# Transposing q's features by DMA instead of on TensorE for four units, and splitting the first expert's weights in two instructions instead of three

## The chip, the cores and the metric

The kernel runs on one core of one Trainium2 chip. The metric is the device time of one execution in microseconds. The kernel before takes 619.28 us (median of 3 runs, 617.71 to 622.87).

In this text PE is TensorE (PEld its weight loads), ACT is ScalarE, DVE is VectorE, POOL is GpSimd, SP is SyncE, which here only issues DMAs.

## The reference

Linear attention with random features feeds a mixture of experts in which each token goes to one expert.

```
phi(x) = exp(h - max h) / sqrt(128),  h = x @ omega.T - |x|^2 / 2    (x scaled by 64^-1/4)
q_p, k_p = phi(q), phi(k)                       # 8 x 8 heads, 576 rows, 128 features
kv  = k_p^T v;   z = sum of k_p over the rows
x   = (q_p kv) / (q_p z + 1e-6)                 # 4608 tokens of 512
e   = argmax(x @ w_gate)                        # one of 8 experts
out = gate * (1 + exp(-x @ w_output_gate[e]))^-1 * (relu(x @ w1[e]) @ w2[e])
```

## The kernel before, in words

The attention is cut into 32 *units*; unit u is one head of two batches, nine chunks of 128 rows, and has a k half and a q half. Four times eight units give the tokens of one quarter; after each quarter the tokens are routed, and *items* (one expert on up to 128 tokens, lines 1661 and 1693) run between the later units and after them.

Matmuls want their operands as pairs of 16-bit halves, a rounded one and a remainder. Units 0 to 7 are `whole`: they project q and k in 32 bits (line 629, two matmuls for each chunk and half; the squares that they need, `lo`, are made by POOL, line 601). From unit 8 on the projection uses halves of x, made by ACT (`hi`, line 544) and POOL (line 551). A projection step `pp` of three chunks fills two PSUM banks; DVE finds a minimum (line 651) and a bias (657, later 660 and 664), and ACT takes the exponentials (670), into `ef`.

The last matmul of a unit, `pn` (line 849), needs q's features transposed, as 16-bit halves, in the tile `et`. There are two ways in the code:

- Units 0 to 7: in three groups of three chunks, PE transposes in 32 bits (`tq`, line 720), ACT rounds out of PSUM (`th`, 725), DVE subtracts (`tl`, 727).
- Units 8 and up: ACT rounds the whole of q's features (`eh`, line 691), POOL subtracts (`el`, 693), into `es`, and one DMA transpose issued by SP brings both halves to `et` (`eT`, line 747).

The first expert's weights are loaded in eight quarters (line 480, 512 KB each) while the first units run. Before, each quarter is scaled in place by ACT (line 484), rounded by ACT (488), and subtracted by POOL (492). Later experts are split by `high` on ACT (line 462, scaled and rounded at once) and `low` on DVE (line 468).

All steps stand in one list written out as numbers (`ORDER`, line 131): every engine, and SP's DMA queue with it, takes its own steps in that order, and a step whose input is late holds all that stand behind it on its engine. `BANKS` lists which PSUM bank each step gets. Tiles rotate through few buffers: two of x (`xt`), v (`rawv`), `es` and `et`, so that a load waits for the last reader of the buffer. On ACT the rounding of unit 8's x (`hi`, line 544) stands ahead of unit 6's key-value halves (`kvh`, line 784), which PE's step `kt` (line 805) waits for through DVE (line 788).

Of the kernel before, what the change touches and what calls it, by code (L numbers as in the profile page):

```python
# [90 lines left out]
WHOLE = 8  # L91
ASSUMED = (4, 12, 21, 26, 31, 37)
# [235 lines left out]
def attention_moe(ctx: ExitStack, tc: tile.TileContext, kqt, kqn, v, om, wg, w1, w2, cf, cm, ci, out):  # L328
    nc = tc.nc
# [1544 lines left out]
```

## Time and profile before

| what | value |
| --- | --- |
| median of 3 runs | 619.28 us (617.71 to 622.87) |
| profiled execution, its own time | 620.54 us |
| its span, first to last instruction | 618.5 us |
| PE busy | 594.8 us (96%) |
| ACT busy | 420.6 us (68%) |
| DVE busy | 386.0 us (62%) |
| POOL busy | 376.2 us (61%) |
| mean granted clock of PE | 0.986 |

The busy times are averages over stages with different limits: the units 0 to 7 fill the first 75 us, the change to the later kind of unit and the first routing the next 45, and from 120 us on items and units share PE. Matmuls are pipelined and their ends are modelled, so a busy PE is not PE at its peak; how long a step holds PE is read from the start of the step after it.

### The profile page before, as it was taken

The page shows a single profiled execution, that of the slowest core. Times are in us where ns is not written, and L with a number is a line of the kernel's source. Part 1 is how long each engine was busy: PE and PEld are TensorE (multiplying, and loading weights), DVE is VectorE, ACT ScalarE, POOL GpSimd, SP SyncE. Part 2 cuts the span into 40 slices and gives each one's busy share as a digit, 9 for nine tenths or more (in the row PEclk, how much of TensorE's full clock was granted, in tenths as well). Part 3 has the DMA queues.
Part 4 walks back from the last instruction along what each step waited for, and adds up shares of the span by engine and source line. Part 5 has one row for each costly group of instructions (what it writes and reads, how often), then busy time and mean ns, then how long its engine had stood idle before and what let it go on. Part 6 is the DMA issues. An engine that isn't in the chain of part 4 may idle for free. (4 is left out here: it accounts for less than half of the span.)

```text
span 618.5 us, 22153 instructions
## 1 busy us (share of the span) xinstructions
PE 594.8 (96%) x8736; PEld 471.3 (76%) x8736; DVE 386.0 (62%) x1220; ACT 420.6 (68%) x978; POOL 376.2 (61%) x275
## 2 busy tenths in 40 slices
PE   8999987999999999999999999999999999999995
PEld 8999876877796777778777777778867587777775
DVE  4877699876678887657797856543693351162143
ACT  6999999779888688889958787872431341351244
POOL 2265689788977879997897889985322122121203
PEclk9999997899999999999999999999999899999999
DMA  8655688999999999989978999777586935942391
GB/s 282 196 158 159 212 274 212 233 236 257 305 251 217 254 281 242 269 188 238 304 199 251 247 192 203 171 170 222 193 176 189 245 82 109 300 117 69 104 278 50
DMA packets 146022, 128.86 MB, mean 208 GB/s; under 512 B 104286, under 2 KB 127584, under 8 KB 144608
## 3 DMA queue, kind: packets, MB, share of 16 engines
q1 hardware_dynamic: 139904, 107.45, 68.6%
q0 software_dynamic: 5984, 19.72, 10.1%
q8 instruction: 73, 1.20, 0.8%
q14 instruction: 61, 0.50, 0.3%
HBM read 83.86 MB, written 19.30 MB: 167 GB/s over the span
## 5 line engine op out<-in xcount | busy, mean ns | idle before, releaser
L1661 PE MATMUL ph<-xt,w1h 128*128 128x128 f16 (+1 forms) x2368 | 200.4, 218 | 2.2 <-ACT ef L670 0.7
L1661 PE MATMUL ph<-xt,w1l 128*128 128x128 f16 (+1 forms) x1184 | 196.6, 218 | 0.9 <-issue 0.9
L1661 PEld LDWEIGHTS <-w1h 128*128 128x128 f16 x2368 | 178.2, 98 | 9.6 <-issue 2.4
L670 ACT ACTIVATE ef<-pp,nb 128x128 f32<-128x128 f32 x576 | 163.7, 397 | 15.7 <-DVE nb L664 11.4
L651 DVE TENSOR_REDUCE pp<-pp 128x3 f32<-128x384 f32 x192 | 103.0, 557 | 35.2 <-PE pp L629 29.0
L693 POOL TENSOR_TENSOR es<-ef,es 128x1152 f16<-128x1152 f32 x44 | 104.8, 2390 | 25.8 <-ACT es L691 15.2
L1661 PEld LDWEIGHTS <-w1l 128*128 128x128 f16 x1184 | 115.2, 98 | 1.6 <-issue 1.6
L1672 DVE SCALAR_TENSOR_TENSOR hl<-ph,hh 128x512 f16<-128x512 f32 (+1 forms) x76 | 50.4, 664 | 95.2 <-ACTq L1555 53.5
L1693 PE MATMUL po<-w2h,hh 128*128 128x512 f16 x280 | 106.9, 382 | 0.4 <-ACT es L691 0.4
L1693 PE MATMUL po<-w2l,hh 128*128 128x512 f16 x280 | 106.8, 382 | 0.0
L1693 PE MATMUL po<-w2h,hl 128*128 128x512 f16 x280 | 106.7, 381 | 0.0
L1668 ACT ACTIVATE hh<-ph 128x512 f16<-128x512 f32 (+1 forms) x76 | 44.5, 591 | 85.5 <-PE ph L1661 65.7
L1693 PEld LDWEIGHTS <-hh 128*128 128x128 f16 x560 | 51.5, 98 | 53.7 <-issue 1.9
L1617 POOL DMA_INDIRECT gx<-rows,gi x38 | 39.5, 1038 | 83.3 <-ACT os L1772 34.4
L551 POOL TENSOR_TENSOR xlo<-xt,xhi 128x1152 f16<-128x1152 f32 x24 | 57.3, 2386 | 9.8 <-ACT xhi L544 8.0
L691 ACT CAST es<-ef 128x1152 f16<-128x1152 f32 x44 | 51.5, 1180 | 3.0 <-DMA et<-es 2.3
L1693 PEld LDWEIGHTS <-hl 128*128 128x128 f16 x280 | 27.5, 98 | 33.8 <-issue 0.8
L1772 ACT ACTIVATE os<-po,gx 128x512 f32<-128x512 f32 (+1 forms) x34 | 23.3, 686 | 43.5 <-PE po L1693 39.7
L849 PE MATMUL pn<-kvs,et 128*128 128x81 f16 (+1 forms) x960 | 47.9, 204 | 2.2 <-DVE nb L664 0.7
L849 PEld LDWEIGHTS <-et 128*128 128x128 f16 (+1 forms) x960 | 40.5, 101 | 9.3 <-issue 1.8
L629 PE MATMUL pp<-omh,xhi 64*128 64x128 f16 x432 | 42.9, 223 | 2.3 <-ACT ef L670 0.9
L1759 POOL DMA_INDIRECT out<-os,oi x25 | 26.6, 1065 | 27.7 <-ACT os L1772 22.9
(215 smaller groups left out, 1093.6 us busy)
## 6 DMA issues: line engine op xcount, KB each, us to landing
r<-w SPq DMA_DIRECT2D x10, 2048.0 KB
xt<-kqt SPq DMA_DIRECT2D x31, 576.0 KB
xn<-kqn SPq DMA_DIRECT2D x24, 576.0 KB
rawv<-v SPq DMA_DIRECT2D x32, 325.0 KB
rows<-xs SPq DMA_DIRECT2D x16, 576.0 KB
r<-w SPq DMA_DIRECT2D x8, 512.0 KB
ef<-w SPq DMA_DIRECT2D x2, 512.0 KB
et<-w SPq DMA_DIRECT2D x2, 512.0 KB
```

What stands on the lines that cost most here:

```text
L551: lambda t0=t0, t1=t1: nc.gpsimd.tensor_tensor(out=xl(u)[:, t0:t1], in0=xt32(u)[:, t0:t1], in1=xh(u)[:, t0:t1], op=ALU.subtract),
L629: nc.tensor.matmul(banks["pp", 2 * u + i, g][:, c, :], x[r, t], w[r, :], start=(a == 0), stop=(a == len(ops) - 1))
L651: nc.vector.tensor_reduce(out=pp[:, 3, 0:3], in_=pp[:, 0:3, :], op=ALU.min, axis=AX.X)
L670: nc.scalar.activation(ef(n)[:, c, :], banks["pp", n, g][:, c % 3, :], AF.Exp, bias=nb(n)[:, c : c + 1], scale=-SK)
L691: nc.scalar.copy(es(slot_es(n))[:, 0], ef(n))
L693: nc.gpsimd.tensor_tensor(out=es(slot_es(n))[:, 1], in0=ef(n), in1=es(slot_es(n))[:, 0], op=ALU.subtract)
L849: nc.tensor.matmul(pn[lo:hi, c - c0, :], a[:, c, lo:hi], w[:, :, b], start=(i == 0), stop=(i == len(ops) - 1))
L1617: nc.gpsimd.indirect_dma_start(out=gx(n), out_offset=None, in_=rows[0 : (j + 1) * NC * P], in_offset=bass.IndirectOffsetOnAxis(ap=tabs[gr] ...
L1661: nc.tensor.matmul(ph[:, f4, 0:w_], w[qd][:, kk, fo : fo + P], xt(n)[:, x, 0:w_], start=(a == 0), stop=(a == 3 * KC - 1))
L1668: nc.scalar.activation(hh(n)[:, sl, 0:w_], banks["ph", n, g][:, :, 0:w_], AF.Relu)
L1672: nc.vector.scalar_tensor_tensor(out=hl(n)[:, sl, 0:w_], in0=banks["ph", n, g][:, :, 0:w_], scalar=0.0, in1=hh(n)[:, sl, 0:w_], op0=ALU.ma ...
L1693: nc.tensor.matmul(po, x(n)[:, f, :], w[f // 2][:, f % 2, :], start=(f == 0 and a == 0), stop=(f == FC - 1 and a == 2))
```

## The change

- Units 2 to 5 (`TURNED`) keep the 32-bit projection, but take the other way to `et`: `tq`, `th` and `tl` go, and `eh`, `el` and `eT` come in their place.
- Each quarter of the first expert's weights is split by `high` (ACT) and `low` (DVE), as the later experts' are; the scaling in place and POOL's subtraction go.
- `ORDER` and `BANKS` are written anew. From the first routing's list of tokens on, the common steps stand in the same order; before it the weights' roundings and subtractions stand earlier, and the `pn` of units 3 and 4 later.

```diff
+TURNED = (2, 3, 4, 5)
...
-        def scale_up(which, i):
-            src, _, _, sc = quarter(which, i)
-            nc.scalar.activation(src, src, AF.Copy, scale=sc)
-
-        def rounded(which, i):
-            src, hi, _, _ = quarter(which, i)
-            nc.scalar.copy(hi, src)
-
-        def remainder(which, i):
-            src, hi, lo, _ = quarter(which, i)
-            nc.gpsimd.tensor_tensor(out=lo, in0=src, in1=hi, op=ALU.subtract)
...
-                    ("w0s", *key), ("ACT",), 0.95, lambda which=which, i=i: scale_up(which, i), after=[("w0", *key)], rank=R
-                )
-                plan.add(
-                    ("w0h", *key), ("ACT",), 0.95, lambda which=which, i=i: rounded(which, i), after=[("w0s", *key)], rank=R
+                    ("w0h", *key), ("ACT",), 0.95, lambda which=which, i=i: high(which, i), after=[("w0", *key)], rank=R
                 )
                 plan.add(
-                    ("w0l", *key), ("POOL",), 2.1, lambda which=which, i=i: remainder(which, i), after=[("w0h", *key)], rank=R
+                    ("w0l", *key), ("DVE",), 1.22, lambda which=which, i=i: low(which, i), after=[("w0h", *key)], rank=R
                 )
...
-        if whole:
+        if whole and u not in TURNED:
             def turned(g):
```

The change's lines lie 13 to 16 above those of before: its 731 is 747, its 677 is 693, its 585 is 601.

SP's queue, from behind the load of unit 5's x, before (578 loads x, 588 loads v, 480 a quarter of the weights, 923 stores rows of the result):

```order
L588 DMA rawv_988<-v 128x650
L578 DMA xt_990<-kqt 128x1152
L480 DMA r_108<-w 128x1024
L578 DMA xt_993<-kqt 128x1152
L923 DMA rows<-xs_547 128x9x128
L923 DMA rows<-xs_1040 128x9x128
L588 DMA rawv_1211<-v 128x650
L578 DMA xt_1213<-kqt 128x1152
L578 DMA xn_1215<-kqn 128x1152
```

and now:

```order
L731 DMA_TRANSPOSE et_663<-es_533 128x18x128
L731 DMA_TRANSPOSE et_910<-es_701 128x18x128
L572 DMA rawv_949<-v 128x650
L562 DMA xt_951<-kqt 128x1152
L479 DMA r_108<-w 128x1024
L562 DMA xt_954<-kqt 128x1152
L731 DMA_TRANSPOSE et_998<-es_846 128x18x128
L907 DMA rows<-xs_542 128x9x128
L907 DMA rows<-xs_992 128x9x128
L572 DMA rawv_1153<-v 128x650
L731 DMA_TRANSPOSE et_1155<-es_987 128x18x128
L562 DMA xt_1157<-kqt 128x1152
```

Unit 2's transpose stands right behind the load of unit 5's x, unit 3's behind that; unit 4's behind the load of unit 7's x, and unit 5's ahead of the load of unit 8's x (`xt_1157`, before `xt_1213`).

POOL, from the squares of unit 4 (`xn_549`) to the remainder of unit 8's x, before (880 and 884 make halves of the result, 902 sums logits):

```order
L902 TENSOR_TENSOR lga_747<-lga_747,xf_833 128x144
L880 CAST xs_1040<-xf_945 128x9x64
L902 TENSOR_TENSOR lga_747<-lga_747,xf_945 128x144
L884 TENSOR_TENSOR xs_1040<-xf_945,xs_1040 128x9x64
L601 TENSOR_TENSOR xn_1049<-xt_993 128x1152
L902 TENSOR_TENSOR lga_747<-lga_747,xf_1109 128x144
L492 TENSOR_TENSOR w2l_105<-r_108,w2h_101 128x1024
L492 TENSOR_TENSOR w1l_95<-r_107,w1h_91 128x1024
L551 TENSOR_TENSOR xlo_1309<-xt_1213,xhi_1243 128x1152
```

and now:

```order
L585 TENSOR_TENSOR xn_995<-xt_951 128x1152
L677 TENSOR_TENSOR es_846<-ef_796,es_846 128x1152
L886 TENSOR_TENSOR lga_727<-lga_727,xf_810 128x144
L864 CAST xs_992<-xf_932 128x9x64
L886 TENSOR_TENSOR lga_727<-lga_727,xf_932 128x144
L868 TENSOR_TENSOR xs_992<-xf_932,xs_992 128x9x64
L585 TENSOR_TENSOR xn_1004<-xt_954 128x1152
L677 TENSOR_TENSOR es_987<-ef_868,es_987 128x1152
L886 TENSOR_TENSOR lga_727<-lga_727,xf_1070 128x144
L535 TENSOR_TENSOR xlo_1251<-xt_1157,xhi_1187 128x1152
```

The remainders of the weights (492) are gone, and a remainder of q's features (677, before 693) follows the squares of units 6 and 7; the two of units 2 and 3 stand in the same way further up, unit 2's right behind the squares of unit 4.

PE, where unit 2's features of q were transposed, between unit 1's `pn` and unit 3's last projection, before:

```order
L849 MATMUL pn_5_565<-kvs_398,et_380 128x81
L720 MATMUL tq_1_578<-ident,ef_413 128x128 x3
L766 MATMUL kv_582<-rawv_326,ef_482 128x130 x5
L720 MATMUL tq_2_588<-ident,ef_413 128x128 x3
L766 MATMUL kv_582<-rawv_326,ef_482 128x130 x5
L629 MATMUL pp_2_625<-omf,xt_328 128x128
```

and now:

```order
L833 MATMUL pn_5_561<-kvs_397,et_380 128x81
L750 MATMUL kv_574<-rawv_326,ef_482 128x130 x10
L613 MATMUL pp_2_609<-omf,xt_328 128x128
L613 MATMUL pp_2_610<-omf,xt_328 128x128
```

The two groups of three transposes are gone and the key-value matmuls (766, now 750) follow each other.

## Rows read from the trace of the kernel before

**Rows 1.** Stretches: length, busy PE PEld DVE ACT POOL, PEclk, DMA share, GB/s.

```profile
10.00:75.00 65.00, 64.76 (x901) 60.03 (x899) 48.52 (x160) 61.70 (x183) 31.21 (x24) 1.00 0.61 190
75.00:120.00 45.00, 37.10 (x544) 32.42 (x545) 40.00 (x171) 39.48 (x118) 37.98 (x25) 0.85 0.87 234
80.00:110.00 30.00, 23.34 (x345) 20.59 (x344) 28.57 (x128) 27.85 (x79) 26.54 (x16) 0.83 0.85 229
95.00:115.00 20.00, 17.16 (x210) 15.22 (x211) 17.12 (x83) 15.83 (x47) 16.84 (x11) 0.66 0.86 220
120.00:600.00 480.00, 473.34 (x6992) 361.55 (x6990) 287.08 (x871) 307.97 (x661) 299.97 (x219) 1.00 0.84 213
```

**Rows 2.** PE in order of time: start, length, line, what, count.

```profile
31.88 0.51 PE L720 MATMUL tq<-ident,ef 128*128 128x128 f32 x3
32.23 1.28 PE L766 MATMUL kv<-rawv,ef 128*128 128x130 f32 x10
...
60.84 0.82 PE L720 MATMUL tq<-ident,ef 128*128 128x128 f32 x6
61.49 0.63 PE L849 MATMUL pn<-kvs,et 128*128 128x81 f16 x12
```

**Rows 3.** Costliest groups by form: count, busy us, mean ns of one, idle before.

```profile
L693 POOL TENSOR_TENSOR es<-ef,es 128x1152 f16<-128x1152 f32 x44 | 104.8, 2390 | 25.8 <-ACT es L691 15.2 <-issue 8.4 <-ACTq L1576 2.1
...
L691 ACT CAST es<-ef 128x1152 f16<-128x1152 f32 x44 | 51.5, 1180 | 3.0 <-DMA et<-es 2.3 <-issue 0.2
...
L468 DVE SCALAR_TENSOR_TENSOR w1l<-r,w1h 128x1024 f16<-128x1024 f32 x16 | 19.6, 1272 | 8.6 <-ACT w1h L462 8.6
...
L727 DVE TENSOR_TENSOR et<-tq,et 128x384 f16<-128x384 f32 x24 | 12.8, 549 | 2.4 <-ACT et L725 2.4
...
L725 ACT CAST et<-tq 128x384 f16<-128x384 f32 x24 | 11.4, 513 | 1.0 <-PE tq L720 1.0
...
L484 ACT ACTIVATE r<-r 128x1024 f32<-128x1024 f32 x8 | 8.8, 1102 | 0.0
L492 POOL TENSOR_TENSOR w1l<-r,w1h 128x1024 f16<-128x1024 f32 x4 | 8.5, 2132 | 0.0
```

**Rows 4.** Queue of SP in order of time: start, length of issue, line, transfer.

```profile
36.36 0.33 SPq L578 DMA_DIRECT2D xt<-kqt  x1
...
55.96 0.33 SPq L578 DMA_DIRECT2D xt<-kqt  x1
...
66.06 0.35 SPq L578 DMA_DIRECT2D xt<-kqt  x1
...
119.17 3.55 SPq L747 DMA_TRANSPOSE et<-es  x1
```

**Rows 5.** DMA engines, 119 to 125 us in 40 slices, busy tenths.

```profile
DMA  0000005999939993996999999999999922991993
```

**Rows 6.** POOL, then ACT, in order of time.

```profile
31.48 2.10 POOL L601 TENSOR_TENSOR xn<-xt 128x1152 f32<-128x1152 f32 x1 [3.65 <-PE pp L629]
...
60.41 2.11 POOL L601 TENSOR_TENSOR xn<-xt 128x1152 f32<-128x1152 f32 x1 [2.28 <-PE kv L766]
...
70.39 1.25 ACT L544 CAST xhi<-xt 128x1152 f16<-128x1152 f32 x1
```

**Rows 7.** PE, then DVE, in order of time.

```profile
43.51 1.34 PE L849 MATMUL pn<-kvs,et 128*128 128x81 f16 x30
...
73.81 0.27 PE L805 MATMUL kv<-cmt,kvs 128*128 128x128 f16 x2
...
76.88 1.03 DVE L651 TENSOR_REDUCE pp<-pp 128x3 f32<-128x384 f32 x2 [1.28 <-PE pp L629]
```

**Rows 8.** POOL at two places, then DVE beside the second.

```profile
169.72 0.48 POOL L902 TENSOR_TENSOR lga<-lga,xf 128x144 f32<-128x144 f32 x1
...
303.22 1.49 POOL L902 TENSOR_TENSOR lga<-lga,xf 128x144 f32<-128x144 f32 x1
...
302.62 5.45 DVE L468 SCALAR_TENSOR_TENSOR w1l<-r,w1h 128x1024 f16<-128x1024 f32 x4 [2.81 <-ACT w1h L462]
```

More of the change, by code (lines that the diff above doesn't have):

```diff
@@ L131 @@
 ORDER = """
[135 rows of a table removed]
[134 rows of a table added]
 """
 BANKS = """
-01234567102453165273016042306751043267430613457425134062356710264573016240615704265137531240763540613710743562347035
-16743510716346571634204765726410356741530274551472630514753026741430621506327140751620461235643154753124567346102751
-06432547130654372164507312506457236105634721406524102364736051244276503270165603257105623715027265703416720614253107
-64623154026731426753126053461752607415236407351406732510467235041672350416273504612357061423353353353353353353353353
-35335335
+01234567102453165273016042307510427430613742514037102655732460615704265137531240763540613710743562347035167435107163
+46571634204765726410356741530274551472630514753026741430621506327140751620461235643154753124567346102751064325471306
+54372164507312506457236105634721406524102364736051244276503270165603257105623715027265703416720614253107646231540267
+3142675312605346175260741523640735140673251046723504167235041627350461235706142335335335335335335335335335335335
 """
```

269 rows, old and new, of the table ORDER are left out of this document.

## The prediction

> **What bounds the kernel now.** I read the busy times by stretch first, then the waits of PE, then the order of time on each queue. From 10 to 75 us PE is busy 64.76 of 65.00 us at full clock, and steps follow each other without a gap [rows 1, 2]: here whatever PE no longer does is time. From 80 to 110 us DVE is busy 28.57 of 30.00 us, PE only 23.34 [rows 1]: the later kind of unit asks more of DVE, the first routing falls in the same place, and DVE is the bound, with ACT close behind (27.85). PE loses 45.00 - 37.10 = 7.9 us idle between 75 and 120 us, and its granted clock falls to a mean of 0.66 between 95 and 115 us, after the stretch in which it waited [rows 1]. From 120 to 600 us PE is busy 473.34 of 480.00 us [rows 1], with the same work before and after the change. So the end moves by as much as the work at 110 to 120 us moves, and the change must be costed up to there.
>
> **The change, part by part.**
>
> *PE's transposes.* Twelve groups of three go. A group holds PE from its start to the next step's: 32.23 - 31.88 = 0.35 us, and two together 61.49 - 60.84 = 0.65 us [rows 2]. Twelve by 0.34 are 4.1 us, all of it in the stretch in which PE is the bound. The 0.51 and 0.82 us that the rows give as lengths overlap the next step and aren't taken.
>
> *ACT.* Eight scalings in place (1.10 us) and twelve roundings out of PSUM (0.51) go, four roundings of 1.18 come: -8.8 - 6.2 + 4.7 = -10.3 us [rows 3]. ACT is busy 61.70 of 65 us up to 75 us, but PE doesn't wait for it there, so I cost this at nothing; the cover is PE's own work. It is slack that the new roundings use.
>
> *POOL.* Eight subtractions of 2.13 us go, four of 2.39 come: -17.0 + 9.6 = -7.5 us [rows 3]. POOL is busy 31.21 of 65 us in the first stretch; nothing for the total. But the four that come stand in a chain to `pn`, which is costed below.
>
> *DVE.* Twelve subtractions of 0.55 us go, eight of 1.27 come: -6.6 + 10.2 = +3.6 us [rows 3]. All stand before 75 us, where DVE is busy 48.52 of 65 us [rows 1]: 16.5 us of slack cover them. What isn't covered is that each, being 1.27 us long, can hold a minimum or bias behind it, and so ACT and a PSUM bank. Bounds: nothing, or 8 by 1.27. I take nothing, since PE has steps of other units to do at each place.
>
> *The new chain to `pn`.* Now q's features go ACT, POOL, SP, DMA. A transpose issued at 119.17 holds SP's queue 3.55 us [rows 4], and the DMA engines fall idle at slice 32 of 40 of a view of 6 us that begins at 119, thus at 123.8 [rows 5]: 4.6 us from issue to landing.
>
> Unit 2: POOL's subtraction stands right behind the squares of unit 4, which ran 31.48 to 33.58 [rows 6], so it ends at 36.0. The queue gets there after the load of unit 5's x, 36.36 before [rows 4], about 1 us sooner now. Issue 36.0, landing 40.6. `pn` started at 43.51 [rows 7]; five groups fewer stand ahead of it, so it is due at 41.8. That fits by a hair, with two loads ahead on the DMA engines. Bounds of the wait: 0 and 1.5 us; I take 0.5.
>
> Unit 5: its transpose stands ahead of the load of unit 8's x on SP. The load of unit 7's x was issued at 55.96 [rows 4], when PE had done unit 5's projection; the squares of unit 7 followed at 60.41 [rows 6], 4.45 us later. Now eight groups (2.7 us) and unit 3's `pn` (1.3 us by unit 2's row [rows 7]) no longer stand ahead of that point, 0.5 us of waiting does: 52.5. Squares from 56.9 to 59.0, subtraction to 61.4, transpose on the queue until 65.0. Unit 8's x was loaded at 66.06 before, and ACT began to round it at 70.39 [rows 4, 6], 4.3 us later; now 65.0 and 69.3, done at 70.5. On ACT that rounding stands ahead of unit 6's key-value halves, which PE's `kt` waits for. `kt` stood at 73.81 [rows 7]; without this it would be due at 73.81 - 4.1 + 0.5 = 70.2, with it at about 71.0 (I allow 0.5 us for the two short steps between). That is 2.8 us sooner than before. Bounds: the load can also be 1.0 us slower beside the transpose's own data, which lands at 66.0.
>
> *Units 3 and 4.* Their `pn` stand later in the new order, behind further projections, so their transposes have some 3 us to spare at the same pace; nothing.
>
> *From there on.* DVE begins its full stretch at 76.88, when the last projection of unit 7 ends [rows 7]. That moves with `kt`, 2.8 us. What DVE does from there to 110 us isn't changed, so its end moves by the same 2.8 us, and so does all that follows. That POOL loses five of its eight weight subtractions from this very stretch helps steps that wait for DVE anyway; nothing.
>
> *Sum.* The profiled execution took 620.54 us: 620.54 - 2.8 = 617.7. The median of the runs, 619.28, stands 1.26 us below that execution, which gives 616.5. Without any stall it is 619.28 - 4.1 = 615.2; with both stalls at their ends (1.0 us more at unit 2, 1.0 more at unit 8) 618.5.
>
> *A rule that speaks against it.* In the trace a logits sum of POOL takes 0.48 us alone and 1.49 us while DVE splits weights, and the four splits beside it take 5.45 us [rows 8]. The Trainium skill's page "GPSIMD Engine Reference", section "8. Key points", says that POOL shares its SBUF interfaces with VectorE and that the two contend when a DVE instruction has two SBUF inputs; such a subtraction has two, and the trace agrees, with 1.0 us more on a short step. By that rule the change puts eight such instructions among the very POOL steps that now lie in the chain; that is the second rival.
>
> **The rivals.**
>
> *The idle stretch shrinks too (faster).* If DVE isn't really the bound from 80 to 110 us, but POOL's lateness with the halves of units 9 to 11 is (POOL 26.54 of 30 [rows 1]), then five subtractions fewer, 5 by 2.13 = 10.7 us, close PE's gaps, and the clock doesn't fall. PE's 17.16 busy us between 95 and 115 us at 0.66 would be 11.3 at full clock: 5.8 us, with the 2.8 above 8.6 us, so 610.7. For it: POOL's load, and that the clock fell only after PE had waited. Against: DVE's 28.57 of 30, which the change leaves as it is.
>
> *SP's queue holds unit 8 (slower).* The price of unit 5's transpose falls on the load behind it. If its subtraction ends after 62.5 (66.06 - 3.55), that load is later than before; from 64.2 on, `kt` is later too, since it had 1.7 us to spare behind the rounding's end at 71.64. By the contention above each of four subtractions or squares in series may take 1.0 us more: 61.4 + 4 = 65.4. Then the load goes out at 69.0, the rounding ends at 74.5, and unit 8's halves are 2.9 us later than before, `kt` 1.2. I take 2.2: 621.5. For it: the chain runs in series through POOL and SP. Against: the single 1.0 us was seen for a short step, and DVE's splits are spread over 50 us.
>
> *DVE takes it all (no change).* The 3.6 us more on DVE, and the wait of minima behind 1.27 us splits, eat the 2.8 us: 619.3. Against: its 16.5 us of slack; for it: PE's banks come free only through DVE and ACT.
>
> **How the numbers follow.** The forecast has 0.54, the faster rival 0.15, the slower one 0.14, no change 0.17. The predicted time is the forecast's, 616.5; its own range is 615.2 to 618.5. The 8 in 10 run from 610.5, where half of the faster rival lies below, to 622.0, which leaves out the worse part of the slower one and a little of the rest. A measurement of this kernel can tell about 1%, 6.2 us, from no change (its three runs lie 5.2 us apart). Faster by that, below 613.1: nearly all of the faster rival and a little of the forecast, 0.16. Slower, above 625.5: only the end of the slower rival, 0.05. The same: 0.79.
>
> **What would show it.** Right: no `tq` of units 2 to 5 and PE still without gaps to 70 us; unit 2's `pn` waiting under 1.5 us for its transpose; the load of unit 8's x issued about 65.0, `kt` of unit 6 about 71.0, DVE's full stretch beginning about 74 and as long as before; the clock falling again. Wrong: a mean clock near 1.00 between 90 and 115 us and PE idle well under 7.9 us (faster rival); the load of unit 8's x after 66 us, or PE waiting for `et` for microseconds (slower rival); gaps on PE behind minima before 70 us (no change).

## The result, and the profile after

The changed kernel takes 628.43 us (median of 6 runs, 627.29 to 635.83) beside 621.74 us of the kernel before (6 runs): a ratio of 1.0143, 95% interval 1.0105 to 1.018. The forecast was 616.5 us with a range of 610.5 to 622.0, that is 0.9955 of the 619.28 us it started from. It is wrong in sign and in size. The profiled execution has a span of 625.2 us (before 618.5) and took 627.29 us.

The kernel before takes 614 us on some chips and 621 on others, so every experiment below is read as its ratio to the runs of before on its own chip, and places in the program are read as time behind one milestone, `kt` of unit 0 (the product that turns a unit's key-value state). Line numbers of other kernels differ by up to 21 from those of before. One profile, that of e7, is of a slower execution; only its part before 101 us is read.

Stretches of the changed kernel (length; busy PE, PEld, DVE, ACT, POOL; PEclk; DMA share; GB/s), which answer to [rows 1]:

```profile
10.00:75.00 65.00, 58.37 (x768) 53.65 (x770) 49.42 (x138) 48.52 (x147) 37.90 (x24) 0.95 0.75 201
75.00:120.00 45.00, 35.23 (x538) 31.09 (x535) 38.32 (x161) 40.58 (x115) 23.84 (x17) 0.92 0.90 249
80.00:110.00 30.00, 23.00 (x375) 19.65 (x374) 27.26 (x107) 27.97 (x77) 20.85 (x16) 1.00 0.90 249
...
120.00:600.00 480.00, 472.54 (x6974) 362.21 (x6973) 290.09 (x892) 309.44 (x672) 305.73 (x223) 1.00 0.85 211
...
45.00:50.00 5.00, 3.54 (x44) 3.33 (x46) 2.99 (x10) 2.88 (x9) 4.25 (x2) 0.66 0.99 190
...
60.00:65.00 5.00, 2.98 (x27) 2.59 (x28) 4.98 (x17) 3.05 (x13) 3.44 (x5) 0.87 1.03 237
65.00:70.00 5.00, 5.00 (x54) 4.76 (x53) 3.15 (x7) 4.30 (x11) 4.70 (x2) 0.79 0.98 273
```

From 10 to 75 us PE is now idle 65.00 - 58.37 = 6.6 us (before 0.24), and its granted clock, which was 1.00 in that stretch, falls to 0.66 and 0.79 in two places, that is, part of the time at 1.2 GHz and not 2.4. ACT is 13 us less busy there, in part because the window now holds less of the program; PE gains nothing by it. PE in order of time, beside [rows 7] (there `pn` of unit 2 stood at 43.51 and `kt` of unit 6 at 73.81):

```profile
41.53 2.51 PE L750 MATMUL kv<-rawv,ef 128*128 128x130 f32 x20
46.46 2.10 PE L833 MATMUL pn<-kvs,et 128*128 128x81 f16 x30 [2.42 <-DMA et<-es]
...
58.30 1.48 PE L833 MATMUL pn<-kvs,et 128*128 128x81 f16 x30
...
62.01 0.84 PE L613 MATMUL pp<-omf,xt 64*128 64x128 f32 x3 [2.16 <-issue]
64.28 3.85 PE L750 MATMUL kv<-rawv,ef 128*128 128x130 f32 x20
...
70.88 0.28 PE L789 MATMUL kv<-cmt,kvs 128*128 128x128 f16 x2
...
80.99 0.27 PE L789 MATMUL kv<-cmt,kvs 128*128 128x128 f16 x2
```

Two stops: 2.42 us at unit 2's `pn`, which waits for the DMA transpose, and 2.16 us before unit 6's projection, of which the view says only "issue". Behind each the clock is low: `pn` takes 2.10 us (1.34 before), unit 5's `kv` 3.85 (2.51 for unit 3's, at 41.53). The last row is unit 6's `kt`, 7.2 us later than before. SP's queue, beside [rows 4]:

```profile
37.05 0.33 SPq L562 DMA_DIRECT2D xt<-kqt  x1
37.49 10.30 SPq L731 DMA_TRANSPOSE et<-es  x2
...
58.23 0.33 SPq L562 DMA_DIRECT2D xt<-kqt  x1
...
69.72 2.66 SPq L731 DMA_TRANSPOSE et<-es  x1
73.22 0.34 SPq L562 DMA_DIRECT2D xt<-kqt  x1
```

Unit 2's transpose is issued at 37.49 and its data is there when `pn` starts, at 46.46: 9.0 us, not 4.6. The last row is the load of unit 8's x, 7.2 us later than before (66.06). Now the milestones, `kt` of each unit as its start behind unit 0's, in us, and unit 0's own start in the trace (worked out from the rows of that product in each trace), with the ratios:

```
        u0 at   u2     u3     u4     u5     u6     u8    ratio to before (95%)
before  21.36  15.08  24.95  32.92  43.06  52.45  72.83  1
after   22.55  14.58  28.19  33.99  48.33  58.44  78.83  1.0143 (1.0105-1.0180)
e1      20.62  14.23  26.64  32.44  46.87  56.56  76.96  1.0080 (1.0051-1.0109)
e2      21.76  15.17  28.28  36.90  47.67  57.16  77.54  1.0077 (1.0044-1.0110)
e3      22.27  14.60  26.05  31.86  48.41  58.69  79.08  1.0090 (1.0059-1.0121)
e4      21.51  14.59  23.74  33.87  48.21  58.32  78.94  1.0087 (1.0054-1.0120)
e5      21.81  14.22  22.86  32.28  45.87  55.58  75.97  1.0075 (1.0049-1.0101)
e6      22.15  14.59  23.50  32.11  45.72  56.32  76.91  1.0075 (1.0041-1.0109)
e7      22.24  15.20  25.55  37.42  48.14  57.65  78.05  1.0083 (1.0054-1.0112)
e8      22.54  14.56  26.23  32.03  49.54  61.16  82.31  1.0166 (1.0124-1.0209)
e9      21.95  14.59  23.36  30.80  42.62  54.43  75.55  1.0100 (1.0054-1.0147)
e10     21.06  14.22  22.42  29.86  41.44  53.36  74.99  1.0112 (1.0074-1.0150)
e11     23.17  15.19  25.88  35.23  50.55  61.02  81.64  1.0174 (1.0115-1.0233)
e12     22.20  14.24  22.43  30.23  41.80  55.24  78.99  1.0113 (1.0080-1.0146)
e13     21.04  14.22  22.43  29.98  41.57  51.21  78.49  1.0101 (1.0068-1.0135)
e14     20.98  14.21  22.43  29.75  41.34  53.96  79.09  1.0120 (1.0088-1.0152)
e15     22.11  14.58  23.09  30.56  42.57  58.48  82.80  1.0196 (1.0154-1.0238)
e16     21.07  14.22  22.82  29.87  41.52  51.21  72.78  1.0023 (0.9991-1.0055)
e17     21.03  14.22  22.85  30.22  42.85  52.91  74.15  1.0040 (1.0007-1.0074)
e18     22.54  14.59  23.46  32.16  43.48  54.02  78.06  1.0077 (1.0049-1.0105)
```

All that the changed kernel loses is lost before unit 6. From unit 6 to unit 8 it takes 20.39 us (before 20.38), and from unit 8 to the end 523.8 us (524.3; both are the span less the start of unit 8's `kt`).

### The profile page after: what moved, and what is told of

It reads as the page before. It is cut to its first block, busy times and chain, and to the rows that moved or that the text cites. A ratio compares the mean times of both kernels' runs of the same rounds, so it can differ in the third digit from the quotient of the medians.

```text
span 625.2 us, 22068 instructions
## 1 busy us (share of the span) xinstructions
PE 592.0 (95%) x8700; PEld 468.8 (75%) x8700; DVE 393.4 (63%) x1216; ACT 415.3 (66%) x962; POOL 374.3 (60%) x271
## 5 line engine op out<-in xcount | busy, mean ns | idle before, releaser
L677 POOL TENSOR_TENSOR es<-ef,es 128x1152 f16<-128x1152 f32 x48 | 114.3, 2391 | 29.5 <-ACT es L675 20.4
L675 ACT CAST es<-ef 128x1152 f16<-128x1152 f32 x48 | 56.2, 1180 | 1.5 <-DMA et<-es 0.7
L833 PE MATMUL pn<-kvs,et 128*128 128x81 f16 (+1 forms) x960 | 49.2, 208 | 4.6 <-DMA et<-es 2.4
L868 POOL TENSOR_TENSOR xs<-xf,xs 128x576 f16<-128x576 f32 x32 | 42.0, 1313 | 1.1
```

Source lines behind the costliest of these rows:

```text
L675: nc.scalar.copy(es(slot_es(n))[:, 0], ef(n))
L677: nc.gpsimd.tensor_tensor(out=es(slot_es(n))[:, 1], in0=ef(n), in1=es(slot_es(n))[:, 0], op=ALU.subtract)
L833: nc.tensor.matmul(pn[lo:hi, c - c0, :], a[:, c, lo:hi], w[:, :, b], start=(i == 0), stop=(i == len(ops) - 1))
L868: nc.gpsimd.tensor_tensor(out=x[:, :, P + o : P + o + D], in0=xf(u)[:, :, 0:D], in1=x[:, :, o : o + D], op=ALU.subtract)
```

## The experiments

The edits of e3 to e18 are in the order in which steps are given to an engine and in the PSUM banks that they get. Both stand in the kernel as tables of numbers, so the diffs name the steps.

**e1 and e2: each half alone.** e1 is the kernel before with the transposes moved to DMA; e2 is the changed kernel with `TURNED = ()`, so only the weights change.

```diff
 # e1, against before
+TURNED = (2, 3, 4, 5)
-        if whole:
+        if whole and u not in TURNED:
 # e2, against the changed kernel
-TURNED = (2, 3, 4, 5)
+TURNED = ()
```

> Half of the change: units 2 to 5 turn q's features by DMA as in the changed kernel, while the first expert's weights are split as before (scaled on ScalarE, rounded on ScalarE, remainder on GpSimd, each at its old place). Theory A (the loss is made where DMA transposes land late and where unit 3's products, moved behind unit 5's projections, leave VectorE's divides standing ahead of unit 5's minima): the loss stays, 625.5 to 629 us. Theory B (the loss comes from the weights' remainders, put on VectorE beside GpSimd and ahead of the minima): the loss goes, 618 to 622 us. Theory C (the transposes hold SP's queue, and the loads behind them are late): the loss stays, 626 to 629 us, and GpSimd's squares of units 6 and 7 stay as late as in the changed kernel.

> The other half: the weights in two instructions (rounding with the scale on ScalarE, remainder on VectorE) at the changed kernel's places, while units 2 to 5 turn q's features on TensorE, as before, and unit 3's products stand at their old place. Theory A: what is lost is the start alone (unit 1's turned state 1.2 us later in the changed kernel, from a remainder that stands ahead of unit 0's transposed halves), 621 to 624 us. Theory B: most of the loss, 625 to 629 us, with VectorE's remainders of 1.22 to 2.5 us ahead of minima. Theory C: no loss, 620 to 622 us.

Each half loses 0.8%, and within the intervals the two add up to the whole. That is A's and C's figure for e1 and B's for e2 (by ratio 626.7 and 626.5 us where before is 621.7); A had given e2 no more than the late start, and C nothing. C's second sign failed: in e1 POOL's squares of units 6 and 7 start at 52.14 and 60.87 us, in the changed kernel at 55.53 and 64.27. e2 shows one place where the weights cost time. DVE, POOL and ACT of e2 in order of time:

```profile
44.17 2.78 DVE L464 SCALAR_TENSOR_TENSOR w1l<-r,w1h 128x1024 f16<-128x1024 f32 x1
```

```profile
43.77 2.11 POOL L582 TENSOR_TENSOR xn<-xt 128x1152 f32<-128x1152 f32 x1 [0.23 <-DMA xt<-kqt]
```

```profile
48.19 1.66 ACT L651 ACTIVATE ef<-pp,nb 128x128 f32<-128x128 f32 x6 [1.52 <-DVE nb L638]
```

The remainder starts at 44.17 while POOL squares until 45.88, and ends at 46.95, that is 1.07 us after POOL is done; alone it takes 1.22. By these times it doesn't run slowly beside POOL, it waits for POOL's instruction to end. Behind it stand unit 4's minima, and ACT waits 1.52 us for their biases.

**e3 and e4: one stop each out of the changed kernel.**

```diff
 # e3, DVE: kvs.4, then
-xf.3 (divides of unit 3, 6 steps), mx.10.1 ... nb.11.1 (minima, biases of unit 5)
+mx.10.1, router's state, ... nb.11.1, xf.3
 # e4, PE                                   # e4, DVE
-pn.2, pp.4.2, kt.3                         -xf.2, mx.9.2 ... nb.8.2
+pp.4.2, kt.3, pn.2                         +mx.9.2 ... nb.8.2, xf.2
```

> The changed kernel with one edit: on VectorE the six steps that divide unit 3's products stand behind the minima and biases of unit 5, not ahead of them; TensorE's order, SP's and ScalarE's are untouched. Theory A: VectorE's idle 3.5 us at 55.8, ScalarE's 3.4 us at 58.1 and TensorE's 2.2 us at 62 go, and with them TensorE's lower clock at 60 to 70: 623.5 to 626.5 us. Theories B and C: 627.5 to 629 us, since the wait is only passed on.

> The changed kernel with one edit: unit 2's products stand behind unit 4's last projection and unit 3's key-value turn on TensorE, and the divides of unit 2 behind unit 4's minima on VectorE. Theory A: TensorE no longer waits 2.4 us for unit 2's transposed features, its clock stays up at 45 to 50, and unit 3's turned state comes 2.5 to 3.5 us earlier: 624 to 626.5 us if the later stop at unit 3 stays, no more than 628 if that stop grows by what was won. Theory B: 627.5 to 629. Theory C: 627.5 to 629, as the loads of units 6 to 8 are issued when they were.

e4 did at its place what theory A said, and more: unit 3 comes 4.45 us earlier (28.19 to 23.74), unit 4 only 0.1. In both, unit 5 is where it was (48.41, 48.21 against 48.33): the next stop took it. The ratios fell by 0.005, and the intervals still overlap with that of the changed kernel. For e4 that is A's second branch; e3 is a miss for A. In e3 four small copies of the router's state came up beside POOL's work. DVE of e3, then POOL:

```profile
54.70 1.57 DVE L392 TENSOR_SCALAR cnt<-cft 128x8 f32<-128x8 f32 x1
56.18 0.16 DVE L393 TENSOR_SCALAR done<-cft 128x8 f32<-128x8 f32 x1
56.26 2.34 DVE L394 COPY off<-cft 128x8 f32<-128x8 f32 x1
```

```profile
54.14 2.11 POOL L580 TENSOR_TENSOR xn<-xt 128x1152 f32<-128x1152 f32 x1 [0.97 <-DMA xt<-kqt]
56.20 2.37 POOL L672 TENSOR_TENSOR es<-ef,es 128x1152 f16<-128x1152 f32 x1
```

Copies of 8 numbers, 0.16 us each where POOL rests, take 1.57 and 2.34 us and end at 56.27 and 58.60, as POOL's instructions end (56.25 and 58.57).

**e5 to e7: all named stops out of e1, of the changed kernel, and one remainder out of e2.** e5 is e1 with both edits of e3 and e4 and the state's copies behind the minima too; e6 is the changed kernel with these and one remainder, w0l.1.2, moved; e7 is e2 with that remainder moved.

```diff
 # e6 and e7, DVE
-gl.2, w0l.1.2, kvs.3, mx.9.0 ... xf.2, w0l.1.3
+gl.2, kvs.3, mx.9.0 ... xf.2, w0l.1.2, w0l.1.3
```

> The transposes alone (weights as before, as in e1_turned_only), with both stops taken out by order alone: unit 2's products behind unit 4's last projection and unit 3's turn on TensorE, unit 2's and unit 3's divides on VectorE behind the minima of units 4 and 5, and the four small copies of the router's state behind them too. e1 lost 2.85 us at unit 2's products (waiting for the transpose) and 2.2 us before unit 6's projections, and after each TensorE ran at its lower clock (the key-value sums of unit 5 took 4.1 us). Theory A (these waits and the clock are the whole loss of this half; its saving on TensorE is real): 5 to 8 us below e1, so 611.5 to 614.5 us, level with the kernel before or up to 2 us faster. Theory C (the transposes' hold on the queue sets the pace): the later milestones stay, 618 to 620 us.

> The changed kernel with the order of e5_turned_unblocked, and the remainder of the weights' third quarter of the first matrix, which stood ahead of unit 4's minima on VectorE while GpSimd was at work, put beside the fourth quarter's, a place where GpSimd is idle. Theory A with B (each half loses by its own waits): what is left is the 1.2 us at the start and the remainders that wait for GpSimd at 63 and 69 us, 614 to 617.5 us. If the order gives nothing more than e3 and e4 gave: 618.5 to 620 us.

> The weights alone (as in e2_weights_only), with one instruction moved: the remainder of the first matrix's third quarter, which took 2.78 us in e2 and stood ahead of unit 4's first minima, goes behind unit 2's last divide, beside the fourth quarter's. In e2 the way from unit 2's turned state to unit 3's took 13.1 us, 3.2 us more than in the kernel before. Theory B (that one instruction, held while GpSimd runs, makes the loss): this way takes 10 to 11.5 us, and the time is 615.5 to 617.5 us. Against it (VectorE's sum of work is what counts, wherever it stands): 618.5 to 620 us.

None gave what A expected: by time e5 came out at C's figure, e6 and e7 at the second of their branches. The milestone of e7 did as expected (unit 2 to unit 3: 10.35 us, e2 13.11), the time didn't: the two remainders, now in a row, took 2.82 us at 49.52, and unit 3 to unit 4 went from 8.6 to 11.9 us. e5 won nothing on e1. Its PE:

```profile
48.50 0.49 PE L623 MATMUL pp<-omf,xt 64*128 64x128 f32 x4 [1.39 <-issue]
...
59.28 0.49 PE L623 MATMUL pp<-omf,xt 64*128 64x128 f32 x4 [1.91 <-issue]
61.34 3.58 PE L760 MATMUL kv<-rawv,ef 128*128 128x130 f32 x20
```

Unit 6's projection starts at 59.28; DVE's last divide of unit 3 ended at 59.18. The table of banks gives this projection the bank which that divide frees (as in the changed kernel, where the divide ran 61.42 to 61.90 and the projection began at 62.01). So the banks became theory D. The sentence on six free banks in e8's expectation counts by the order in the table; in time most of them weren't free yet, since ACT's exponentials were late too, as e8 then showed.

**e8 to e11: banks chosen anew** for the requests of units 3 to 6 (longest free first, a bank freed by a divide last), in the changed kernel, in e6, e5 and e7. A few later requests follow from these.

```diff
 # e8, bank of          (freed by)
-pp.12.0  5             (xf.3, DVE)
+pp.12.0  one that an exponential freed (ACT)
```

> The changed kernel, every engine's order as it is; only the PSUM banks that the steps of units 3 to 6 take are chosen anew: of the free banks the one that has been free longest, and one that a divide frees only if no other is free. In the changed kernel unit 6's first projections took the bank that unit 3's last divide freed (61.90 us, projections at 62.01), although six others had been free for up to 4 us, and unit 5's first ones a bank of unit 2's divide. Theory D (TensorE stops since the table of banks, made for the old order, hands it banks that late divides free): the 2.16 us before unit 6's projections go in part, unit 5's turned state 1 to 3 us earlier, 625 to 627 us where before is 621.7. Theory A (VectorE's divides ahead of the minima are what stops): no change, since the exponentials are late either way, 1.012 to 1.015 of the time before.

> e6_all_unblocked (the changed kernel with unit 2's products later, the divides of units 2 and 3 behind the minima, one remainder moved) with banks chosen as in e8_banks_only. Theory A with D (orders and banks each hid behind the other): no stop of TensorE over 1 us between 40 and 75 us but the one of unit 2, the clock stays up, and unit 8's turned state stands 72.5 to 74.5 us behind unit 0's (before 72.8, e6 76.9): 1.000 to 1.004 of the time before. If the milestone stays at 76 to 77: 1.006 to 1.009.

> e5_turned_unblocked (transposes alone, products and divides moved) with banks chosen as in e8_banks_only. e5 had 1.39 us of stop before unit 5's projections and 1.91 us before unit 6's, each ending as a divide freed a bank, and 2 to 3 us of lower clock behind them. Theory A with D: those go, unit 8's turned state 70.5 to 72.5 us behind unit 0's (before 72.8, e5 76.0): 0.994 to 1.000 of the time before. If the transposes themselves hold the pace: 1.006 to 1.009 as e5.

> e7_one_remainder_moved (weights alone, one remainder moved) with banks chosen as in e8_banks_only. In e7 unit 4's key-value sums waited 2.00 us for a bank that VectorE freed behind two remainders (49.5 to 52.3), and then ran at the lower clock (4.07 us). Theory B with D: this stop goes, unit 8's turned state 73.5 to 76 us behind unit 0's (before 72.8, e7 78.0): 1.001 to 1.005. If VectorE's added work alone sets the pace: 1.007 to 1.009 as e7.

Theory D falls: alone the new banks don't help. e11 is slower than e7, and e8, though its interval overlaps that of the changed kernel, has unit 6 2.7 us later. By ratio all four came out above both branches of what was expected. In e8 unit 6's projection stops 2.98 us, now for a bank of ACT's, as ACT's exponentials stand behind the blocked minima. With the order mended as well, unit 5 comes 41.44 us behind unit 0 in e10 and 42.62 in e9, before 43.06: up to here the transposes alone win 1.6 us, where e1 lost 3.8. The stops form a chain: minima wait behind divides on DVE, exponentials on ACT wait for the minima, banks for the exponentials, and PE for the banks. So all must go together. But unit 8 is 2.2 us late again in e10, which expected 70.5 to 72.5, and 2.7 in e9. Its SP, then its ACT:

```profile
63.04 3.94 SPq L741 DMA_TRANSPOSE et<-es  x1
67.07 0.53 SPq L572 DMA_DIRECT2D xt<-kqt  x1
```

```profile
72.64 1.15 ACT L538 CAST xhi<-xt 128x1152 f16<-128x1152 f32 x1 [3.80 <-DMA xt<-kqt]
```

**e12 to e15: the queue and the rounding of unit 8's x.**

```diff
 # e12, SP                                  # e13, ACT
-eT.5, ld.t.8, ld.n.8                       -hi.8, kvh.6, th.6.2
+ld.t.8, ld.n.8, eT.5                       +kvh.6, th.6.2, hi.8
 # e14: e10 with both.  e15: e9 with both.  All four: banks by e8's rule up to unit 8.
```

> e10_turned_unblocked_banks (transposes alone, no stops before 65 us) with one edit on SP's queue: unit 5's DMA transpose goes behind the loads of unit 8's x and its squares, not ahead of them (the banks are chosen by e10's rule up to unit 8, so that unit 7's projections no longer wait for a transposed half). In e10 the load was issued at 67.07, after 3.94 us that the transpose held the queue, though unit 6's last projection, whose buffer it takes, was done at 64.4; it landed at 72.6, and ScalarE waited 3.80 us for it with unit 6's key-value copies behind. Theory C (the queue): load issued at 64.5 to 65.5, landed near 70, unit 8's turned state 72 to 73.5 us behind unit 0's (e10 75.0, before 72.8); 2 to 3 us less than e10. If the transpose then lands too late for unit 5's products: 75 or more.

> e10_turned_unblocked_banks with one edit on ScalarE: the rounding of unit 8's x stands behind unit 6's key-value copy and second transposed third, not ahead of them (and GpSimd's remainder of it likewise; banks as in e12_queue). Theory E (what takes the gain back is ScalarE's in-order queue, held 3.80 us by a load): unit 6's turned state comes 1 to 2.5 us earlier, and unit 8's 72.5 to 74 us behind unit 0's (e10 75.0). If unit 8's projections wait for the rounded halves anyway: 74.5 to 75.5.

> The transposes alone with every stop that the traces named taken out: e12_queue's and e13_round_later's edits together. If stops by order were the whole cost of this half, its saving of 4.1 us on TensorE before 70 us must now show: unit 8's turned state 69.5 to 72 us behind unit 0's (before 72.8), the time 0.993 to 1.000 of the kernel before. If other work takes it back (the 75 to 125 us stretch, bound by VectorE): 1.002 to 1.008.

> The changed kernel with both edits of e14_turned_all on top of e9_all_unblocked_banks, so the whole change with every stop that the traces named taken out, except the remainders on VectorE that wait for GpSimd at 63 and 69 us and the one of 1.2 us at the start. Unit 8's turned state 72 to 74 us behind unit 0's, which itself is 1.0 to 1.2 us late: 0.998 to 1.005 of the kernel before. If VectorE's remainders cost by their sum: 1.007 to 1.012.

e12 came out at its second branch: behind the loads the transposed data come too late. SP, then PE of e12:

```profile
66.81 6.41 SPq L741 DMA_TRANSPOSE et<-es  x1
```

```profile
75.35 2.29 PE L843 MATMUL pn<-kvs,et 128*128 128x81 f16 x30 [3.09 <-DMA et<-es]
```

The transpose lands 8.5 us after its issue, and PE waits 3.09 us, as it does in e15 (3.10) and, by 2.57, in e14. e13 is the opposite: with the rounding behind `kvh.6`, unit 6 comes 51.21 us behind unit 0, 1.24 us ahead of the kernel before; theory E holds up to there. Then it lost 7 us, to its banks as e16 shows; the longest stop is this one on PE:

```profile
92.19 0.23 PE L623 MATMUL pp<-omh,xhi 64*128 64x128 f16 x2 [3.47 <-ACT ef L664]
```

So e14 and e15, which missed by far, are spoiled by the bank rule as well, and say nothing on the change's worth. The same may hold for e9 to e11 behind unit 6; that wasn't tested.

**e16 and e17: the banks of the changed kernel kept** wherever the same step frees them; only the first projections of the k halves of units 5 and 6 are given others, and six requests follow from that. So e16 is e5 with eight other banks and the rounding moved. e17 also leaves unit 5 on PE.

```diff
 # e16: e13 with the old table's banks, but for pp.10.0, pp.12.0 (and six that follow)
 # e17: e16 with
-TURNED = (2, 3, 4, 5)
+TURNED = (2, 3, 4)
```

> e13_round_later with the banks of the changed kernel's own table wherever a step can take the bank that the same step freed there; only the first projections of units 5 and 6 take others (those that an exponential frees, not a divide), and eight requests follow from that. Theory F (from unit 6 on e12 to e15 lost by the bank table that they were given): the stops of 0.92 and 3.47 us at 77 and 92 us go; unit 6's turned state 51 to 52 us, unit 8's 72.5 to 74.5 us behind unit 0's (e13 78.5, before 72.8), 1.000 to 1.005 of the kernel before. If unit 8's late x sets the pace whatever the banks: 75 us or more, 1.006 to 1.010.

> As e16_banks_kept, but only units 2, 3 and 4 turn q's features by DMA; unit 5 keeps TensorE, ScalarE and VectorE for it, as before, so that nothing stands on SP's queue ahead of the load of unit 8's x. Theory C (the queue and the late x8 are what is left): the load is issued within 1 us of unit 6's last projection and unit 8's turned state is 70.5 to 72.5 us behind unit 0's (before 72.8): 0.994 to 1.000 of the kernel before. If the DMA queues are busy with loads and transposes anyway: 73 to 75 us, 1.000 to 1.005.

e16 came as expected: 1.0023, not to be told from the kernel before. It isn't faster either. No run puts its order, its banks or its moved rounding into a kernel that turns on PE, so what they alone are worth isn't known. Stretches of e16:

```profile
10.00:75.00 65.00, 62.67 (x878) 57.97 (x879) 44.01 (x149) 60.60 (x173) 40.03 (x28) 1.00 0.80 228
75.00:120.00 45.00, 36.50 (x530) 31.57 (x528) 39.98 (x170) 39.40 (x117) 38.80 (x26) 0.85 0.93 241
80.00:110.00 30.00, 23.00 (x338) 20.27 (x337) 28.04 (x129) 27.45 (x77) 26.50 (x16) 0.82 0.99 238
```

It keeps PE's clock at 1.00 to 75 us; from 80 to 110 us DVE and ACT are as full as before [rows 1]. It is 1.24 us ahead of the kernel before at unit 6 and 0.05 at units 7 and 8 (the kernel before has unit 7 at 61.75, e16 at 61.70). e17 answers theory C: with no transpose ahead of it on the queue the load goes out 0.7 us sooner (66.17, e16 66.88), and from unit 5 to unit 8 it takes 31.3 us as e16 does (before 29.8): its second branch. Unit 5's transpose on the queue isn't what takes the last 1.2 us.

**e18: e16 with the weights in two instructions.**

```diff
 # e18, against e16: w0s, w0h on ACT and w0l on POOL become
+w0h (scale and round) on ACT, w0l on DVE, at e6's places
```

> The whole change (transposes, and the weights in two instructions with the remainder on VectorE) in the order and with the bank rule of e16_banks_kept; of the eight remainders one is moved to a place where GpSimd is idle, as in e6. If the weights' half lost only by the one remainder that stood ahead of unit 4's minima and by the banks: unit 8's turned state 72.5 to 73.5 us behind unit 0's, the time 1.002 to 1.005, what is left being the 1.2 us at the start. If each remainder that meets GpSimd at work, and the 1.22 us that each takes ahead of other VectorE work, is paid for: 74.5 to 76 us, 1.006 to 1.010.

1.0077 against e16's 1.0023: the weights' half keeps a price. By ratio that is the second branch, but unit 8, 78.06 us behind unit 0, is later than both branches had it. Unit 0 stands at 22.54 us, and the eleven kernels with the new weights have it at 22.25 on average, the eight with the old ones and the kernel before at 21.24 (21.36, 20.62, 21.81, 21.06, 22.20, 21.04, 20.98, 21.07, 21.03): 1.0 us. In the changed kernel the first remainder stands on DVE ahead of unit 0's transposed halves (17.47 to 18.69 us; these begin at 18.61, before at 17.41). The rest builds up to unit 8. DVE, POOL and SP of e18:

```profile
63.87 2.48 DVE L462 SCALAR_TENSOR_TENSOR w2l<-r,w2h 128x1024 f16<-128x1024 f32 x1
```

```profile
63.16 2.10 POOL L580 TENSOR_TENSOR xn<-xt 128x1152 f32<-128x1152 f32 x1
65.23 3.34 POOL L672 TENSOR_TENSOR es<-ef,es 128x1152 f16<-128x1152 f32 x1
```

```profile
68.60 2.66 SPq L726 DMA_TRANSPOSE et<-es  x1
71.36 0.54 SPq L557 DMA_DIRECT2D xt<-kqt  x1
```

The remainder waits for POOL's squares (to 65.26) and ends at 66.35; POOL's next subtraction waits for it and ends at 68.57; the transpose and the load of unit 8's x follow in line, 4.5 us later than in e16 (3.0 us as counted from unit 0). How much of e18's price is this chain and how much the other seven remainders wasn't told apart.

## Why the prediction was wrong

PE does less, as forecast, but the rest of the program didn't follow: the prediction failed at unit 2's wait, which it sized too small, and at two terms that it put at nothing, units 3 and 4 and DVE's remainders.

- **PE's 4.1 us.** The direction is right, the term too large. From unit 0's `kt` to unit 6's the kernel before takes 52.45 us, with PE busy 52.35; e16 takes 51.21, with PE busy 49.80. So without the twelve groups PE is busy 2.55 us less, 0.2 us for each and not 0.34. Why a group is worth less than its time to the next step stays open.
- **Unit 2's wait, taken as 0.5 with bounds 0 to 1.5: failed.** It was 2.42 us. The transpose was issued 1.5 us later than forecast (37.49, not 36.0), but the step that was mis-sized is its landing. The forecast took 4.6 us from issue to landing, from a transpose with a quiet queue [rows 5]; behind three loads issued in the 1.8 us before it, this one took 9.0 us (e12: 8.5 behind two). In e1, from 40 to 45 us, the DMA engines are busy all the time and move 164 GB/s, against 280 before when as busy (60 to 65 us).
- **"Units 3 and 4 ... nothing": the step that failed worst.** I looked at the transposes, which had time to spare, and not at who waits for `pn`. Unit 3's stood behind further projections on PE (58.30, before 51.48), but its divides stood where they were on DVE, ahead of unit 5's minima, and a bank of its went to unit 6's projection. DVE and ACT of the changed kernel:

```profile
55.47 0.31 DVE L772 SCALAR_TENSOR_TENSOR kvs<-kv,kvs 128x130 f16<-128x130 f32 x1 [0.57 <-ACT kvs L768]
59.25 0.17 DVE L842 TENSOR_SCALAR den<-pn 128x5 f32<-128x5 f32 x1 [3.47 <-PE pn L833]
...
61.42 0.48 DVE L846 TENSOR_TENSOR xf<-pn,den 128x320 f32<-128x320 f32 x1
```

```profile
61.54 0.88 ACT L654 ACTIVATE ef<-pp,nb 128x128 f32<-128x128 f32 x3 [3.40 <-DVE nb L641]
```

DVE waits 3.47 us for `pn`, ACT 3.40 for the minima behind it, PE 2.16 for the divide's bank. Up to unit 5 e10, and to the end e16, show that this and unit 2's wait, with what follows from them, were the loss of the transposes' half: with order and banks mended, and in e16 the rounding moved, it is gone.

- **DVE's +3.6 us at nothing: failed.** "PE has steps of other units to do at each place" isn't so: e2, with the weights' half alone, loses 0.8%. That the remainders on DVE make this loss is read from the traces; ACT's roundings, which stand earlier in the new order, were not tested apart from them. The slack of 16.5 us was a sum over the stretch, and the remainders stood ahead of minima. Nor was 1.27 us the length: the changed kernel's DVE and POOL have

```profile
43.60 2.46 DVE L467 SCALAR_TENSOR_TENSOR w1l<-r,w1h 128x1024 f16<-128x1024 f32 x1 [0.64 <-ACT w1h L461]
```

```profile
42.60 2.37 POOL L677 TENSOR_TENSOR es<-ef,es 128x1152 f16<-128x1152 f32 x1 [0.33 <-ACT es L675]
44.93 3.09 POOL L585 TENSOR_TENSOR xn<-xt 128x1152 f32<-128x1152 f32 x1
```

DVE waits until POOL's subtraction ends (44.97), POOL's squares until DVE ends (46.06; 2.10 us alone, row 31.48 of [rows 6]). I had given this to a rival of 0.14 and priced it on POOL alone, at 1.0 us per step, which is what POOL's squares show; DVE's wait had no price. The contention that the Trainium skill's "GPSIMD Engine Reference", section "8. Key points", names agrees with these rows.

- **Unit 8's load, forecast for 65.0.** It went out at 73.22, which with PE's 2.42 us for `et` gives both signs of the slower rival. In the changed kernel that is a follower, for unit 5 was already 6.5 us late. The second rival's mechanism is real but came second: with the other stops out, e10 has it (67.07, ACT waiting 3.80 us). Its time, 621.5, was too small, since it held this one stop and none of those before it.
- **What moves rigidly.** Right for a delay: unit 6 to unit 8 and all behind are unchanged. Wrong for a gain: in e16 1.24 us of lead at unit 6 are 0.05 at unit 7. Its time is that of the rival "no change", but not by that rival's mechanism, which was the weights on DVE. Unit 5's transpose doesn't take the lead back (e17). The trace of e16 shows part of what does, though no run tests it; POOL, SP, ACT and PE:

```profile
73.32 2.38 POOL L545 TENSOR_TENSOR xlo<-xt,xhi 128x1152 f16<-128x1152 f32 x1 [3.95 <-ACT xhi L538]
...
75.73 0.80 SPq L572 DMA_DIRECT2D xt<-kqt  x2
...
80.99 1.15 ACT L538 CAST xhi<-xt 128x1152 f16<-128x1152 f32 x1 [0.64 <-DMA xt<-kqt]
...
82.77 0.27 PE L799 MATMUL kv<-cmt,kvs 128*128 128x128 f16 x2 [0.85 <-DVE kvs L782]
```

With the rounding moved, POOL's remainder of unit 8's x ends at 75.70 (before 74.11). The loads of units 10 and 9 stand in that order on SP; unit 10's takes the buffer that this remainder reads, so it goes out at 75.73, and unit 9's behind it. ACT waits 0.64 us for unit 9's x, ahead of unit 7's key-value halves, and PE waits 0.85 us ahead of unit 7's `kt`, where the kernel before waits 0.36. That is 0.5 of the 1.2 us; the rest stays open.

- **The faster rival.** What it started from came: from 75 to 120 us POOL is busy 23.84 us (before 37.98), and the clock's mean is 0.92 (0.85). What it was to win didn't: PE is idle 9.8 us there (7.9), DVE is nearly as full from 80 to 110 us (27.26, before 28.57), and from unit 8 to the end only 0.5 us is won. That POOL's lighter load gives nothing, as the forecast had it, is borne out.
- **The clock.** It had no term below 75 us. Behind the stops of 2.42 and 2.16 us it fell to means of 0.66 and 0.79 (over 5 us), behind the 1.91 us of e5 to 0.55 (60 to 62 us). By idle time and by busy time multiplied by the missing share of clock, the changed kernel's PE loses 5.2 + 2.6 us between 20 and 80 us, the kernel before 0.6 + 0.

## What to carry to other kernels

When a step moves later on an engine, follow what is queued for its result on the next engines, and which buffers it hands back to whom: work that stands behind it in order waits, however much slack the sums show. Take a DMA's time to landing from a place where the queues are as full as where it will stand. And where stops follow one another, taking one out shows little or nothing in the end time (e3 to e6); compare milestones, and take them all out before judging the change (e16).

## What the runs showed of the hardware

- Some of DVE's instructions take turns with POOL's subtractions and squares, by whole instructions: the weights' remainders (1.22 us alone) took 2.46, 2.48 and 2.78 us, copies of 8 numbers with one input (0.16) took 1.57 and 2.34, and POOL's took 3.09 (2.10) and 3.34 (2.39). That their data lie in SBUF isn't the whole condition. In the kernel before, reciprocals of 5 numbers in SBUF ran beside POOL at their usual length (0.18 us at 82.95, inside a subtraction from 82.30 to 84.67), and so did sums over 128x1152 in SBUF (1.34 us at 79.44) and minima out of PSUM (0.56).
- A DMA transpose of 18 blocks held SP's queue for 2.46 us (e3, at 58.60) to 6.41 us (e12), and landed 8.5 to 9.0 us after its issue behind two or three loads.
- The clock didn't fall behind every stop of that length: in e1 PE waited 2.85 us before 44.41 and had 1.00 from 45 to 50 us. I have no explanation that the runs bear out.
